# A streaming attention and channel-mix kernel: two units loaded at the start, sink values by a matmul, three PSUM banks for the channel mix, mixtures in two steps

## The chip, the cores and the metric

One Trainium2 chip, one core. The metric is the device time of one launch in microseconds; the kernel before is given as the median of three runs. The trace shows the engines TensorE (PE, its weight loads as PEld), VectorE (DVE), ScalarE (ACT), GpSimd (POOL) and the queue engine SyncE (SP). TensorE's granted clock is one of two levels, 1.2 or 2.4 GHz; the profile shows it as 0.5 or 1.0.

## What is computed

Attention in which each query sees the first 4 positions (the sinks) and the last 128 positions, and behind it a channel mix with a token shift:

```python
# q, k, v: (4, 8, 768, 64) = (batch, heads, sequence, head size)
keep = (pos_k < 4) | ((pos_q - pos_k >= 0) & (pos_q - pos_k < 128))
a = softmax(where(keep, q @ k.T / 8, -1e9))
x = heads_side_by_side(a @ v)              # (4, 768, 512)
x_prev = x shifted by one position
xk = mu_k * x + (1 - mu_k) * x_prev
xr = mu_r * x + (1 - mu_r) * x_prev
kk = relu(xk @ w_k) ** 2                   # w_k: 512 x 1024
out = sigmoid(xr @ w_r) * (kk @ w_v)       # w_r: 512 x 512, w_v: 1024 x 512
```

## The kernel before

The work is cut into 12 units of 256 positions, three to a batch entry (T = 0, 1, 2), each unit into four pairs of heads. The main loop runs over n = 4 * unit + pair. The order of every engine's instructions is the order in which they are written.

One pass of the loop issues `scores(n)` (L190: keys times queries into the two-bank tile `sc`; ScalarE takes the exponential, L194, into `e`), every second pass `mix`, then `masked(n)` (VectorE multiplies `e` by a 0/1 mask, L200 or L203), `values(n - 1)` (L216 for the sinks, L227 for the window, into the tile `o`; VectorE divides into `x`, L231 and L232), `prepare(u + 1, part)` (TensorE transposes keys or queries of the next unit, L151, ScalarE copies them out, L154; GpSimd casts the values of v, L156), and, in between, two or three chunks of the channel mix of an earlier unit (`fill`, `ffn`). `mix` (two halves a unit) transposes `x` (L247), copies it to `xt` (ACT, L253), takes the difference to the previous position `td` (L255) and makes two slices of `xk` and two of `xr` (L261), all one behind the other on VectorE.

The channel mix of a unit is 10 chunks: four of `xk @ w_k` (L274; ReLU on ACT, L278, square on DVE, L279), two of `xr @ w_r` (L286, tanh L289), and twice two halves of `kk @ w_v` (L294), each pair closed by the product `o_sb` on DVE (L299) and a store. In this text f0 to f3 are the first four chunks, r0 and r1 the next two, v0a, v0b, v1a, v1b the last four. Their results go to eight `mm` tiles a unit, which take turns in two PSUM banks. PSUM has eight banks here: two for `sc`, two for `tps` (all transposes and the sink scores), two for `o`, two for `mm`.

The unit lag is such that f0 of unit u runs in pass 4u + 6, one pass behind the second half of `mix` of that unit, and the `o_sb` of the unit before it are in pass 4u + 5.

At the start, unit 0 is loaded by SP (six loads of 256 KB in pieces of 256 bytes, L69), then eight small loads (L110) bring the sink rows of v, all batches, to `vs4`; then unit 1 is loaded. `w_k` is loaded by GpSimd's queue early, `w_r` and `w_v` behind the first work of unit 0. In pass 4 VectorE halves `w_v` into `wv_h` (L348, eight instructions). The sink rows of v are spread to `vsink` by GpSimd once a batch entry (L163).

Of the kernel before, what the change touches and what calls it, by code (L numbers as in the profile page):

```python
# [17 lines left out]
def kernel(  # L18
# [14 lines left out]
    nc = tc.nc  # L33
    B, H, S, D = q.shape
# [95 lines left out]
    hmask = const.tile([32, H, D + 1], FP32, name="hmask")  # L130
# [10 lines left out]
    def prepare(u, part):  # L141
        b, T = divmod(u, NT)
        ks, qs, vs = raw[u]
        g = part % 2
        if part == 0:
            kts[u] = kt_pool.tile([128, 2, NP, 128], BF16, name="kt")
            qts[u] = kt_pool.tile([128, NP, 256], BF16, name="qt")
        src, dst = ((ks, kts[u][:, g, :, :]), (qs, qts[u][:, :, 128 * g:128 * g + 128]))[part // 2]
        ps = tr_ps.tile([128, NP, 128], FP32, name="tps")
        for c in range(NP):  # L150
            nc.tensor.transpose(out=ps[:, c, :],  # L151
                                in_=src[:, g, 2 * c:2 * c + 2, :].rearrange("p a d -> p (a d)"),
                                identity=ident32)
# [3 lines left out]
        if part == 2 and T == 0:  # L157
# [78 lines left out]

    mixed = {}

    def mix(u, half):
# [11 lines left out]
        cur = xt[:, c0:c0 + 2, t0:t0 + 256]  # L251
        prv = xt[:, c0:c0 + 2, t0 - 1:t0 + 255]
        nc.scalar.copy(out=cur, in_=ps)  # L253
        td = x_pool.tile([128, 2, 256], BF16, name="td")
        nc.vector.tensor_tensor(out=td, in0=cur, in1=prv, op=ALU.subtract)  # L255
        if half == 0:
            mixed[u] = (x_pool.tile([128, NC, 256], BF16, name="xk"),
                        x_pool.tile([128, NC, 256], BF16, name="xr"))
        for dst, mu in zip(mixed[u], (mu_k_sb, mu_r_sb)):
            for i in range(2):  # L260
                nc.vector.scalar_tensor_tensor(  # L261
                    out=dst[:, c0 + i, :], in0=td[:, i, :], scalar=mu[:, c0 + i:c0 + i + 1],
                    in1=prv[:, i, :], op0=ALU.mult, op1=ALU.add)
# [50 lines left out]
    def fill(n, count=1):
        if n >= LAG:
            for _ in range(count):
                next(chunks, None)

    with tc.manual_schedule():
        for part in range(4):  # L320
            prepare(0, part)
        load(1)
        nc.gpsimd.dma_start(out=wr_sb, in_=moe_w_r.rearrange("(c p) f -> p c f", p=128))
        nc.gpsimd.dma_start(out=wv_sb, in_=moe_w_v.rearrange("(c p) f -> p c f", p=128))
        for n in range(N + LAG):
# [5 lines left out]
            if 2 <= n < N + 2 and c % 2 == 1:
                mix((n - 2) // NP, ((n - 2) % NP) // 2)
            fill(n)
            if n < N:
# [52 lines left out]
```

## Time and profile before

| | before |
|---|---|
| runs | 222.0, 222.08, 222.2 us, median 222.08 |
| profiled execution | 222.13 us, of which 220.4 us from first to last instruction |
| PE busy | 180.1 us (82%) |
| DVE busy | 140.9 us (64%) |
| ACT busy | 124.9 us (57%) |
| POOL busy | 34.4 us (16%) |
| chain that ended last | PE 50%, DVE 16%, ACT 12%, DMA 11%, SP's queue 5%, issue 4% |

PE is busy most of the time, but the shares are means over two stages that differ: the first 40 us, in which loads decide, and the rest, in which a unit follows a unit. An idle time in the trace has behind it the instruction that ended it.

### The profile page before, as it was taken

How to read it: one execution, taken by the hardware profiler on the slowest of the kernel's cores; microseconds unless marked ns; L12 is line 12 of the kernel's file. 1: busy time of each engine (PE TensorE's matmuls, PEld its weight loads, DVE VectorE, ACT ScalarE, POOL GpSimd, SP SyncE). 2: the span in 40 equal slices, each digit the busy share in tenths (PEclk: the TensorE clock that was granted, in tenths of full speed). 3: DMA queues.
4: the chain of work that ended last, by engine and by line, in shares of the span. 5: the costliest groups of instructions: out<-in, count | busy, mean ns of one | idle time of the engine just before them, and what ended most of it. 6: DMA issues, size and time to landing. Idle time of an engine off the chain costs nothing.

```text
span 220.4 us, 4299 instructions
## 1 busy us (share of the span) xinstructions
PE 180.1 (82%) x1664; PEld 120.9 (55%) x1664; DVE 140.9 (64%) x344; ACT 124.9 (57%) x201; POOL 34.4 (16%) x69
## 2 busy tenths in 40 slices
PE   1705706999898898996997998988998989979892
PEld 1403405675765755854755757657557557555550
DVE  0011634976786678659669757857866696697632
ACT  2402703694675675774764956855757748555250
POOL 8736011223002001032020020050020200000000
PEclk9999985799999999999999999999999999999998
DMA  7979999950591991951782945915908911020202
GB/s 128 213 142 220 179 221 209 221 97 3 146 202 37 218 166 49 216 120 49 179 157 97 206 83 150 210 26 154 222 24 213 156 49 48 3 95 0 75 23 95
DMA packets 81668, 28.10 MB, mean 127 GB/s; under 512 B 76528, under 2 KB 78064, under 8 KB 81648
## 3 DMA queue, kind: packets, MB, share of 16 engines
q1 hardware_dynamic: 78496, 25.20, 52.6%
q0 software_dynamic: 2096, 2.62, 6.9%
q8 instruction: 13, 0.21, 0.4%
q10 hardware_dynamic: 1056, 0.00, 0.3%
q14 instruction: 7, 0.06, 0.1%
HBM read 24.15 MB, written 6.29 MB: 138 GB/s over the span
## 4 chain that ended last, share of the span: by engine, by line
PE 50%; DVE 16%; ACT 12%; DMA 11%; SPq 5%; issue 4%; ACTq 0%; DVEq 0%
PE mm L274 19%; PE mm L286 9%; DMA ks<-in_k_dram 6%; PE tps L151 6%; PE mm L294 6%; DVE xr L261 5%; SPq L69 4%; DMA vs<-in_v_dram 4%; ACT e L194 4%; DVE xk L261 4%; DVE o_sb L299 3%; PE sc L190 3%; ACT xt L253 3%; ACT rl L278 3%; DVE td L255 3%
## 5 line engine op out<-in xcount | busy, mean ns | idle before, releaser
L274 PE MATMUL mm<-xk,wk_sb 128*128 128x256 bf16 x384 | 50.1, 275 | 12.9 <-DVE o_sb L299 8.5
L194 ACT ACTIVATE e<-sc 128x1024 bf16<-128x1024 f32 (+1 forms) x48 | 46.0, 958 | 9.0 <-PE sc L190 9.0
L294 PE MATMUL mm<-wv_h,kk 128*128 128x512 bf16 x192 | 48.3, 379 | 0.0
L274 PEld LDWEIGHTS <-wk_sb 128*128 128x128 bf16 x384 | 36.4, 98 | 19.1 <-issue 14.6
L278 ACT ACTIVATE rl<-mm 128x512 bf16<-128x512 f32 x48 | 29.1, 607 | 29.2 <-PE mm L274 29.2
L156 POOL CAST v<-vs 128x512 bf16<-128x512 f32 x24 | 15.9, 664 | 139.5 <-DMA vs<-in_v_dram 83.7
L154 ACT CAST kt<-tps 128x512 bf16<-128x512 f32 x24 | 14.1, 586 | 41.5 <-PE tps L151 41.5
L255 DVE TENSOR_TENSOR td<-xt 128x512 bf16<-128x512 bf16 x24 | 10.6, 440 | 40.1 <-ACT xt L253 40.1
L151 PE MATMUL tps<-ident,ks 128*128 128x128 f32 x96 | 17.4, 312 | 20.1 <-DMA ks<-in_k_dram 20.1
L151 PEld LDWEIGHTS tps<-ident,ks 128*128 128x128 f32 x96 | 13.4, 161 | 24.3 <-issue 15.3
L286 PE MATMUL mm<-wr_sb,xr 128*128 128x512 bf16 x96 | 24.4, 380 | 0.0
L294 PEld LDWEIGHTS <-kk 128*128 128x128 bf16 x192 | 16.9, 98 | 13.1
L261 DVE SCALAR_TENSOR_TENSOR xk<-td,mu_k_sb,xt 128x256 bf16<-128x256 bf16 x48 | 23.2, 524 | 0.9
L279 DVE TENSOR_TENSOR kk<-rl 128x512 bf16<-128x512 bf16 x48 | 20.2, 421 | 5.4 <-ACT rl L278 3.9
L227 PE MATMUL o<-v,e 128*128 128x65 bf16 x352 | 21.0, 196 | 1.9 <-DVE e L203 1.3
L203 DVE TENSOR_TENSOR e<-e,mask 128x768 bf16<-128x768 bf16 x16 | 8.8, 551 | 21.5 <-ACT e L194 21.5
L200 DVE TENSOR_TENSOR e<-e,mask 128x1024 bf16<-128x1024 bf16 x32 | 22.3, 697 | 0.0
L261 DVE SCALAR_TENSOR_TENSOR xr<-td,mu_r_sb,xt 128x256 bf16<-128x256 bf16 x48 | 21.7, 492 | 0.0
L227 PEld LDWEIGHTS <-e 128*128 128x128 bf16 x352 | 17.7, 99 | 7.0 <-DVE e L200 1.9
L232 DVE TENSOR_TENSOR x<-o,rec 128x256 bf16<-128x256 f32 x48 | 20.4, 424 | 1.6
L190 PE MATMUL sc<-qt,kt 64*128 64x128 bf16 (+1 forms) x256 | 19.1, 251 | 0.7 <-ACT qt L154 0.7
L299 DVE SCALAR_TENSOR_TENSOR o_sb<-th,mm 128x512 f32<-128x512 f32 x24 | 16.2, 678 | 3.5 <-PE mm L294 3.5
(42 smaller groups left out, 166.6 us busy)
## 6 DMA issues: line engine op xcount, KB each, us to landing
ks<-in_k_dram SPq DMA_DIRECT2D x24, 256.0 KB
qs<-in_q_dram SPq DMA_DIRECT2D x24, 256.0 KB
vs<-in_v_dram SPq DMA_DIRECT2D x24, 256.0 KB
out_dram<-o_sb SPq DMA_DIRECT2D x24, 256.0 KB
wk_sb<-in_moe_w_k_dram POOLq DMA_DIRECT2D x1, 1024.0 KB, 9.7
wv_sb<-in_moe_w_v_dram POOLq DMA_DIRECT2D x1, 1024.0 KB, 13.9
wr_sb<-in_moe_w_r_dram POOLq DMA_DIRECT2D x1, 512.0 KB, 7.9
vs<-in_v_dram SPq DMA_DIRECT2D x8, 4.0 KB
```

The costliest lines, as they stand in the source:

```text
L151: nc.tensor.transpose(out=ps[:, c, :], in_=src[:, g, 2 * c:2 * c + 2, :].rearrange("p a d -> p (a d)"), identity=ident32)
L190: nc.tensor.matmul(out=sc[:, a, o0:o1], lhsT=lhs[rows], rhs=qt[rows, c, q0:q0 + o1 - o0], start=True, stop=True)
L194: nc.scalar.activation(out=e[:, :, lo:], in_=sc[:, :, lo:], func=AF.Exp, scale=scale)
L200: nc.vector.tensor_tensor(out=e, in0=e, in1=mask.rearrange("p a g k q -> p a (g k q)"), op=ALU.mult)
L227: nc.tensor.matmul(out=o[:, g, a, :], lhsT=e[:, a, e0:e0 + 128], rhs=rhs, start=(T == 0 and i == 0), stop=(i == len(blocks) - 1), skip_gro ...
L232: nc.vector.tensor_tensor(out=xs[u][:, :, 128 * c:128 * c + 128].rearrange("p g (a d) -> p g a d", a=2), in0=o[:, :, :, 0:D], in1=rec.to_b ...
L261: nc.vector.scalar_tensor_tensor(out=dst[:, c0 + i, :], in0=td[:, i, :], scalar=mu[:, c0 + i:c0 + i + 1], in1=prv[:, i, :], op0=ALU.mult, ...
L274: nc.tensor.matmul(out=ps[:, i, :], lhsT=wk_sb[:, c, 128 * f:128 * f + 128], rhs=xk[:, c, :], start=(c == 0), stop=(c == NC - 1), skip_gro ...
L278: nc.scalar.activation(out=rl, in_=ps, func=AF.Relu)
L286: nc.tensor.matmul(out=ps, lhsT=xr[:, c, 128 * g:128 * g + 128], rhs=wr_sb[:, c, :], start=(c == 0), stop=(c == NC - 1))
L294: nc.tensor.matmul(out=ps, lhsT=kk[:, f, 128 * g:128 * g + 128], rhs=wv_h[:, f, :], start=(f == 0), stop=(f == NF - 1))
L299: nc.vector.scalar_tensor_tensor(out=o_sb, in0=th[g], scalar=1.0, in1=ps, op0=ALU.add, op1=ALU.mult)
```

## The change

SP loads units 0 and 1 one behind the other; the eight small loads are gone. The sink rows of v are taken from the cast values of unit T = 0 of each batch entry: a matmul with a 0/1 matrix `spread` copies rows 0 to 3 of all heads to 32 rows in a `tps` bank, and VectorE multiplies them by `hmask` into `vsink` (`sink_values`), in place of GpSimd's L163. `o` has one bank and `mm` three. `mix` is split: `transposed` (PE and ACT) stands where `mix` stood, `td` and `xk` follow `values` of the same pass, and `xr` follows one pass later. The four parts of `prepare(1)` run together in pass 3 in place of one a pass, the copies to `ksink` are made in part 3 in place of 2, `wr_sb` and `wv_sb` are asked for at the end of pass 0, and `wv_h` is made in pass 5 in place of 4.

```diff
-    o_ps = ctx.enter_context(tc.tile_pool(name="o_ps", bufs=2, space=PSUM))
-    mm_ps = ctx.enter_context(tc.tile_pool(name="mm_ps", bufs=2, space=PSUM))
+    o_ps = ctx.enter_context(tc.tile_pool(name="o_ps", bufs=1, space=PSUM))
+    mm_ps = ctx.enter_context(tc.tile_pool(name="mm_ps", bufs=3, space=PSUM))
...
     load(0)
+    load(1)
...
-    for h in range(H):
-        nc.sync.dma_start(out=vs4[4 * h:4 * h + 4, :, 0:D],
-                          in_=v[:, h, 0:NS, :].rearrange("b s d -> s b d"))
...
+    def sink_values(b):
+        ps = tr_ps.tile([128, H, D], FP32, name="tps")
+        nc.tensor.matmul(out=ps, lhsT=spread, rhs=v_bufs[b * NT % 3][:, 0, :, 0:D],
+                         start=True, stop=True)
+        nc.vector.tensor_tensor(out=vsink[b % 2][0:32, :, 0:D], in0=ps[0:32], op=ALU.mult,
+                                in1=hmask[:, :, 0:D])
...
+            if c % 2 == 1 and 2 <= n < N + 2:
+                transposed((n - 2) // NP, ((n - 2) % NP) // 2)
+            if n >= 6:
+                fill()
+            if inner:
                 masked(n)
             if 1 <= n < N + 1:
                 values(n - 1)
+            if c % 2 == 1 and 2 <= n < N + 2:
+                mix((n - 2) // NP, ((n - 2) % NP) // 2, 0)
+            if n >= 6:
+                fill()
+            if inner and u + 1 < U:
+                if u == 0 and c == 3:
+                    for part in range(4):
+                        prepare(1, part)
+                elif u > 0:
+                    prepare(u + 1, c)
                 if c == 3 and u + 2 < U:
                     load(u + 2)
+            if c % 2 == 0 and 3 <= n < N + 3:
+                mix((n - 3) // NP, ((n - 3) % NP) // 2, 1)
+            if c == 2 and inner and u % NT == 0:
+                sink_values(u // NT)
```

What this moves is seen in three places. The first is VectorE at the border of two units, in the pass in which unit u - 1 ends its channel mix: `o_sb`, then the mask `e`, `rec` and `x`, then the second `o_sb`, and `kk` of f0. Before:

```order
L232 TENSOR_TENSOR x<-o,rec 128x2x128
L255 TENSOR_TENSOR td<-xt_140 128x512
L261 SCALAR_TENSOR_TENSOR xk<-td,mu_k_sb,xt_140 128x256 x2
L261 SCALAR_TENSOR_TENSOR xr<-td,mu_r_sb,xt_140 128x256 x2
L299 SCALAR_TENSOR_TENSOR o_sb<-th,mm 128x512
L200 TENSOR_TENSOR e<-e,mask 128x1024
L231 RECIPROCAL rec<-o 128x4
L232 TENSOR_TENSOR x<-o,rec 128x2x128
L299 SCALAR_TENSOR_TENSOR o_sb<-th,mm 128x512
L279 TENSOR_TENSOR kk<-rl 128x512
```

And with the change (the line numbers are those of the changed kernel):

```order
L277 SCALAR_TENSOR_TENSOR xr<-td,mu_r_sb,xt_140 128x256 x2
L315 SCALAR_TENSOR_TENSOR o_sb<-th,mm 128x512
L207 TENSOR_TENSOR e<-e,mask 128x1024
L238 RECIPROCAL rec<-o 128x4
L239 TENSOR_TENSOR x<-o,rec 128x2x128
L273 TENSOR_TENSOR td<-xt_140 128x512
L277 SCALAR_TENSOR_TENSOR xk<-td,mu_k_sb,xt_140 128x256 x2
L315 SCALAR_TENSOR_TENSOR o_sb<-th,mm 128x512
L295 TENSOR_TENSOR kk<-rl 128x512
```

The first `o_sb` stood behind `td`, `xk` and `xr`; now it stands ahead of `td` and `xk`, and the `xr` ahead of it is that of the other half. The `xr` of this half comes two rows of `kk` later.

The second place is TensorE at f0 of a unit, with what its instructions wait for. Before:

```order
L274 LDWEIGHTS wk_sb
L274 MATMUL mm<-xk,wk_sb 128x256 [waits DVE_49]
L274 LDWEIGHTS wk_sb
L274 MATMUL mm<-xk,wk_sb 128x256
L274 LDWEIGHTS wk_sb
```

With the change:

```order
L290 MATMUL mm<-xk,wk_sb 128x256
L290 LDWEIGHTS wk_sb
L290 MATMUL mm<-xk,wk_sb 128x256
L290 LDWEIGHTS wk_sb
L290 MATMUL mm<-xk,wk_sb 128x256 [waits DVE_49]
L290 LDWEIGHTS wk_sb
L290 MATMUL mm<-xk,wk_sb 128x256 [waits DVE_49]
```

The wait on VectorE stood at f0's first matmul, which needs a bank that `o_sb` empties; now it stands at the third and the fourth, which need the two `xk` slices of the second half.

The third place is VectorE in passes 4 to 6. Before:

```order
L200 TENSOR_TENSOR e<-e,mask 128x1024
L231 RECIPROCAL rec<-o 128x4
L232 TENSOR_TENSOR x<-o,rec 128x2x128
L348 TENSOR_SCALAR wv_h<-wv_sb 128x512 x8
L255 TENSOR_TENSOR td<-xt_140 128x512
```

With the change:

```order
L273 TENSOR_TENSOR td<-xt_140 128x512
L277 SCALAR_TENSOR_TENSOR xk<-td,mu_k_sb,xt_140 128x256 x2
L376 TENSOR_SCALAR wv_h<-wv_sb 128x512 x8
L295 TENSOR_TENSOR kk<-rl 128x512
L207 TENSOR_TENSOR e<-e,mask 128x1024
L238 RECIPROCAL rec<-o 128x4
```

The eight `wv_h` instructions stood ahead of the second half of `mix` of unit 0; now they stand between it and the first `kk`.

## Rows read from the trace of the kernel before

**Rows 1.** The page's first line.

```profile
span 220.4 us, 4299 instructions
```

**Rows 2.** Waits of the whole run: us in total, times, longest us.

```profile
DVE td L255 <- ACT xt L253: 40.1, 24, 3.1
...
PE tps L151 <- DMA ks<-in_k_dram: 20.1, 4, 8.2
...
PE mm L274 <- DVE o_sb L299: 8.5, 11, 1.4
...
PE mm L274 <- ACT rl L278: 4.4, 10, 0.6
```

**Rows 3.** Busy time by engine in one unit, from f1 to f1.

```profile
72.73:87.97 15.24, 14.29 (x138) 9.81 (x138) 11.28 (x29) 10.39 (x17) 1.24 (x2) 1.00 0.69 139
```

**Rows 4.** Timeline, VectorE at a border of units: start us, us.

```profile
67.94 0.43 DVE L255 TENSOR_TENSOR td<-xt 128x512 bf16<-128x512 bf16 x1 [1.78 <-ACT xt L253]
...
68.40 1.11 DVE L261 SCALAR_TENSOR_TENSOR xk<-td,mu_k_sb,xt 128x256 bf16<-128x256 bf16 x2
...
69.43 0.87 DVE L261 SCALAR_TENSOR_TENSOR xr<-td,mu_r_sb,xt 128x256 bf16<-128x256 bf16 x2
...
70.22 0.67 DVE L299 SCALAR_TENSOR_TENSOR o_sb<-th,mm 128x512 f32<-128x512 f32 x1
70.82 0.54 DVE L203 TENSOR_TENSOR e<-e,mask 128x768 bf16<-128x768 bf16 x1
...
71.29 0.17 DVE L231 RECIPROCAL rec<-o 128x4 f32<-128x4 f32 x1
71.49 0.42 DVE L232 TENSOR_TENSOR x<-o,rec 128x256 bf16<-128x256 f32 x1
...
73.73 0.42 DVE L232 TENSOR_TENSOR x<-o,rec 128x256 bf16<-128x256 f32 x1
```

**Rows 5.** Timeline, TensorE at the same border.

```profile
66.53 1.03 PE L294 MATMUL mm<-wv_h,kk 128*128 128x512 bf16 x4
...
69.83 0.34 PE L190 MATMUL sc<-qt,kt 64*128 64x256 bf16 x4
70.95 1.03 PE L274 MATMUL mm<-xk,wk_sb 128*128 128x256 bf16 x8 [0.78 <-DVE o_sb L299]
...
72.73 1.03 PE L274 MATMUL mm<-xk,wk_sb 128*128 128x256 bf16 x8 [0.56 <-ACT rl L278]
...
74.40 0.40 PE L247 MATMUL tps<-ident,x 128*128 128x128 bf16 x4
```

**Rows 6.** Timeline, GpSimd and VectorE, where GpSimd writes vsink.

```profile
99.07 1.43 POOL L163 TENSOR_TENSOR vsink<-hmask,vs 32x520 bf16<-32x520 f32 x1
99.49 1.70 DVE L261 SCALAR_TENSOR_TENSOR xk<-td,mu_k_sb,xt 128x256 bf16<-128x256 bf16 x2
```

**Rows 7.** Timeline, GpSimd's cast of v at the border of rows 4.

```profile
67.28 1.56 POOL L156 CAST v<-vs 128x512 bf16<-128x512 f32 x2 [14.11 <-DMA vs<-in_v_dram]
```

**Rows 8.** Stretches of 2 us: PE, PEld, DVE, ACT, POOL; PEclk, DMA share, GB/s.

```profile
12.00:14.00 2.00, 0.00 (x0) 0.00 (x0) 0.17 (x1) 0.00 (x0) 0.00 (x0) 1.00 1.19 253
14.00:16.00 2.00, 0.00 (x0) 0.00 (x0) 0.00 (x0) 0.00 (x0) 1.64 (x3) 1.00 0.20 35
16.00:18.00 2.00, 0.00 (x0) 0.00 (x0) 0.00 (x0) 0.00 (x0) 1.86 (x5) 1.00 0.71 162
```

**Rows 9.** Timeline, SP's queue: the small loads, and unit 2's first.

```profile
6.90 8.49 SPq L110 DMA_DIRECT2D vs<-in_v_dram  x8
...
20.88 10.68 SPq L69 DMA_DIRECT2D ks<-in_k_dram  x2
```

**Rows 10.** Timeline, VectorE and TensorE where unit 2's keys arrive.

```profile
28.13 0.36 PE L227 MATMUL o<-v,e 128*128 128x65 bf16 x6 [1.29 <-DVE e L203]
...
33.15 2.12 DVE L348 TENSOR_SCALAR wv_h<-wv_sb 128x512 bf16<-128x512 bf16 x8 [3.38 <-DMA wv_sb<-in_moe_w_v_dram]
...
35.12 1.09 PE L151 MATMUL tps<-ident,ks 128*128 128x128 f32 x4 [6.63 <-DMA ks<-in_k_dram]
```

More of the change, by code (lines that the diff above doesn't have):

```diff
@@ L129 @@
         nc.gpsimd.memset(t, 0.0)
-    hmask = const.tile([32, H, D + 1], FP32, name="hmask")
+    hmask = const.tile([32, H, D + 1], BF16, name="hmask")
     nc.gpsimd.memset(hmask, 1.0)
@@ L135 @@
                             pattern=[[4, H], [0, D + 1]], channel_multiplier=-1)
-    nc.gpsimd.memset(vs4[:, :, D:D + 1], 1.0)
+    for t in vsink:
+        nc.gpsimd.tensor_copy(out=t[0:32, :, D:D + 1], in_=hmask[:, :, D:D + 1])
+    spread = const.tile([128, 128], BF16, name="spread")
+    nc.gpsimd.memset(spread, 0.0)
+    nc.gpsimd.tensor_copy(out=spread[0:NS, 0:4 * H].rearrange("p (h s) -> p h s", s=NS),
+                          in_=ident[0:NS, 0:NS].unsqueeze(1).to_broadcast([NS, H, NS]))
     kts, qts = {}, {}
@@ L156, in prepare @@
             nc.gpsimd.tensor_copy(out=v_bufs[u % 3][:, g, :, 0:D], in_=vs[:, g, :, :])
-        if part == 2 and T == 0:
+        if part == 3 and T == 0:
             kz = ksink[b % 2].rearrange("p (c w) -> p c w", w=136)
@@ L162, in prepare @@
                                       in_=kts[u][rows, 0, :, 0:NS])
-            nc.gpsimd.tensor_tensor(
-                out=vsink[b % 2][0:32, :, :], op=ALU.mult, in0=hmask,
-                in1=vs4[:, b:b + 1, :].to_broadcast([32, H, D + 1]))
+    def sink_values(b):
[4 more added lines that the diff above has]
+                                in1=hmask[:, :, 0:D])
     es, xs, live = {}, {}, {}
@@ L237, with transposed @@
     mixed = {}
-    def mix(u, half):
+    def transposed(u, half):
         b, T = divmod(u, NT)
@@ L250, in mix @@
         t0 = 2 + 256 * T
-        cur = xt[:, c0:c0 + 2, t0:t0 + 256]
+        nc.scalar.copy(out=xt[:, c0:c0 + 2, t0:t0 + 256], in_=ps)
+    def mix(u, half, which):
+        b, T = divmod(u, NT)
+        xt = xts[b % 2]
+        c0 = 2 * half
+        t0 = 2 + 256 * T
         prv = xt[:, c0:c0 + 2, t0 - 1:t0 + 255]
[L253 to L256, printed above, removed]
+        if half == 0 and which == 0:
             mixed[u] = (x_pool.tile([128, NC, 256], BF16, name="xk"),
[L258 to L263, printed above, removed]
+                        x_pool.tile([128, NC, 256], BF16, name="xr"),
+                        x_pool.tile([128, NC, 256], BF16, name="td"))
+        td = mixed[u][2][:, c0:c0 + 2, :]
+        if which == 0:
+            nc.vector.tensor_tensor(out=td, in0=xt[:, c0:c0 + 2, t0:t0 + 256], in1=prv,
+                                    op=ALU.subtract)
+        dst, mu = mixed[u][which], (mu_k_sb, mu_r_sb)[which]
+        for i in range(2):
+            nc.vector.scalar_tensor_tensor(
+                out=dst[:, c0 + i, :], in0=td[:, i, :], scalar=mu[:, c0 + i:c0 + i + 1],
+                in1=prv[:, i, :], op0=ALU.mult, op1=ALU.add)
     def ffn(u):
         b, T = divmod(u, NT)
-        xk, xr = mixed[u]
+        xk, xr, _ = mixed[u]
         kk = kk_pool.tile([128, NF, 256], BF16, name="kk")
@@ L310, with fill @@
     chunks = stream()
-    LAG = 6
     N = U * NP
[L314 to L319, printed above, removed]
+    def fill(count=1):
+        for _ in range(count):
+            next(chunks, None)
+    ORDERED = None
+    with tc.manual_schedule(engines=ORDERED):
         for part in range(4):
             prepare(0, part)
[L322 to L325, printed above, removed]
+        for n in range(N + 6):
             u, c = divmod(n, NP)
-            if n < N:
+            inner = n < N
+            if inner:
                 if c == 0 and u % NT > 0:
@@ L330 @@
                 scores(n)
[L331 to L334, printed above, removed]
+            if c % 2 == 1 and 2 <= n < N + 2:
+                transposed((n - 2) // NP, ((n - 2) % NP) // 2)
+            if n >= 6:
+                fill()
+            if inner:
                 masked(n)
@@ L337 @@
                 values(n - 1)
-            fill(n)
-            if n < N and u + 1 < U:
-                prepare(u + 1, c)
+            if c % 2 == 1 and 2 <= n < N + 2:
[8 more added lines that the diff above has]
+                    prepare(u + 1, c)
                 if c == 3 and u + 2 < U:
                     load(u + 2)
-            if c % 2:
-                fill(n)
-            if n == 4:
+            if c % 2 == 0 and 3 <= n < N + 3:
+                mix((n - 3) // NP, ((n - 3) % NP) // 2, 1)
+            if c == 2 and inner and u % NT == 0:
+                sink_values(u // NT)
+            if c % 2 and n >= 6:
+                fill()
+            if n == 0:
+                nc.gpsimd.dma_start(out=wr_sb, in_=moe_w_r.rearrange("(c p) f -> p c f", p=128))
+                nc.gpsimd.dma_start(out=wv_sb, in_=moe_w_v.rearrange("(c p) f -> p c f", p=128))
+            if n == 5:
                 for f in range(NF):
```

1 line of the change is left out of this document (removed).

## The prediction

> **What bounds the kernel now.** I read the list of waits first, then the timeline at one border of two units, then the first 40 us in stretches of 2 us.
>
> From about 42 us on, the profile repeats unit by unit. In the unit from f1 to f1 that the table by engine shows, TensorE is busy 14.29 of 15.24 us [rows 3]; VectorE has 11.28 and ScalarE 10.39, so TensorE is the bound and 0.95 us a unit is idle. The list of waits says where: f0 and f1 wait for `o_sb` 8.5 us in 11 waits and for the ReLU 4.4 us in 10 [rows 2]. Together that is 12.9 us, at eleven borders of units. The timeline of one border shows the mechanism. v0b ends at 66.53 + 1.03 = 67.56 us [rows 5], but its `o_sb` starts at 70.22, because VectorE first does `td`, `xk` and `xr`, and `td` itself had waited 1.78 us for ScalarE's copy into `xt` [rows 4]. f0 needs the bank that this `o_sb` empties and waits 0.78 us; f1 needs the bank of the second `o_sb` and the ReLU and waits 0.56 [rows 5]. The 40.1 us for which `td` waits for `xt` [rows 2] are VectorE's idle time with work standing behind it.
>
> The first 35 us are another stage. TensorE's last work before the gap starts at 28.13, and it goes on at 35.12, when the keys of unit 2 have landed, after 6.63 us of waiting [rows 10], one of four waits for keys with 20.1 us in all [rows 2]. The transfer engines are busy all that time (share 1.19 from 12 to 14 us) but for a hole: 0.20 from 14 to 16 and 0.71 from 16 to 18 [rows 8]. The hole is where SP had been held for 8.49 us by the eight small loads, until 15.4 us [rows 9], so that unit 1 was asked for only when unit 0 had landed.
>
> **The change, part by part.**
>
> *Third bank and split mixtures: minus 12.9.* With three banks f0 takes a bank that was emptied long before, f1 the one that the first `o_sb` empties, f2 that of the second. f1 starts 0.87 us of matmuls and more after f0, so both named waits go: -12.9 us.
>
> *What is late next: f0's third and fourth matmul, +2.6.* They need `xk` of the second half, which now stands behind `o_sb`, mask, `rec`, `x` and `td`. From v0b's end: `o_sb` to mask 0.60, mask to `rec` 0.47, `rec` to `x` 0.20, `x` 0.42, `td` to `xk` 0.46, a pair of such mixtures 0.87 (the `xr` pair; the `xk` pair beside it was disturbed), and two hand-overs of 0.06 (`o_sb` ends at 70.89, f0 starts at 70.95) [rows 4, 5]. That is 3.14 us, so `xk` is whole at 70.70. TensorE is through with the scores at 69.83 + 0.34 = 70.17 [rows 5], and the fourth matmul of a chunk of eight in 0.87 us comes 0.33 later, at 70.50. The wait is 0.20 us; the third matmul, whose slice is done about 0.42 earlier, does not wait. In units with sinks both sides are somewhat longer, and I take 0.20 for ten borders. Where the last units have no `prepare` between v1a and v1b, some 0.4 us of cover is missing, so 0.60 for one: 10 x 0.20 + 0.60 = 2.6 us. The bounds are 0 (a shorter path) and 0.6 at each border (6.6).
>
> *The transposes behind f1: +2.0.* Their second pair needs `x`, and the chain to it (f0, ReLU, `kk`, mask, `rec`, `x`) does not get shorter: f0 starts at 70.95, `x` ends at 73.73 + 0.42 = 74.15, that is 3.20 later [rows 4]. TensorE needs from f0 to the transposes 74.40 - 70.95 - 0.56 = 2.89 us without f1's wait [rows 5], and the second pair comes about 0.1 after that. So f1's old wait had covered some 0.2 us, which now shows: 10 x 0.20 = 2.0 us. Bounds: 0 and 0.4 each.
>
> *The sink values: +0.75, and a gain already counted.* The trace has no such matmul; four of 512 columns take 1.03 us [rows 5], so one is at most 0.26, with no TensorE work beside it: 3 x 0.25 = 0.75 us for the three after the start. Below, 0.2 each; above, 0.5, if the weight load shows. The VectorE product (nearest: `x` 0.42 and `o_sb` 0.67 [rows 4]) stands behind `xr`, in a place with 1 us of slack; without that cover it costs up to 0.67 each. GpSimd's product goes: while it ran (1.43 us), the pair of `xk` took 1.70 in place of 0.87 [rows 6], and this 0.83 is part of the longest wait for `o_sb`, 1.4 us [rows 2]; it is in the 12.9.
>
> The GPSIMD Engine Reference of the Trainium skill (Key points) says that GpSimd shares its SBUF interfaces with VectorE and contends with instructions that have two SBUF inputs. Rows 6 agree, and so do rows 4 and 7: `xk` took 1.11 while a cast of v ran. By the rule the casts, which stay, go on costing, so the border chain would be 0.24 longer, the rival B below.
>
> *One bank for `o`: 0.* `values(n)` must now wait until VectorE has read `values(n - 1)`. In the pass at the border, `x` follows the mask that `values(n)` needs anyway by 0.62 us (`rec` and `x` [rows 4]), and the next `values` stand behind a chunk of 0.87 and, as a rule, `prepare`, scores and another chunk, about 3 us. I find at least 1 us of slack in each of the four passes of a unit. Uncovered, it would cost 0.62 plus two hand-overs, some 0.7 us a pass.
>
> *The start: -1.5.* With load(1) directly behind load(0) the hole closes: (1.19 - 0.20) x 2 + (1.19 - 0.71) x 2 = 2.9 us at share 1.19, or 2.5 us of full work [rows 8]. If the rest of the traffic is the same, unit 2's keys land at about 32.6 in place of 35.12. Running the four parts of `prepare(1)` together costs nothing: before, TensorE had begun the last of that work at 28.13 [rows 10], 4.5 us ahead of the new time of those keys, and it has no more to do now. But `wv_h`, 2.12 us on VectorE [rows 10], was hidden in TensorE's wait; now it stands between `xk` and the first `kk`, ahead of the mask and `x` that the transposes of pass 7 need. I give back 1.0 of the 2.5 for it. Bounds: 0 (all 2.1 us shown, and 0.4 lost elsewhere) and -2.5. GpSimd's initial work changes by some tenths, under its wait for v.
>
> **Sum.** 220.4 [rows 1] - 12.9 + 2.6 + 2.0 + 0.75 - 1.5 = 211.35 us of span. The profiled execution took 222.13 us, 1.73 more than its span; the runs' median is 222.08, so they agree. 211.35 + 1.73 = **213.1 us**.
>
> **Rivals.**
>
> A. *Less comes back than I fear.* No new waits at f0 or the transposes, and all of the hole: 220.4 - 12.9 + 0.75 - 2.5 + 1.73 = 207.5 us. Against it: both waits come out of rows, with little room.
>
> B. *The VectorE chain takes most of it.* The casts of v collide with the border chain (1.11 against 0.87 [rows 4, 7]), so f0 waits 0.45 at each of eleven borders (5.0), the transposes 0.4 at ten (4.0), and the start gives nothing because `wv_h` shows in full: 220.4 - 12.9 + 5.0 + 4.0 + 0.75 + 1.73 = 219.0 us.
>
> C. *The one bank for `o` decides.* Perfetto Trace Analysis of the Trainium skill (Matmuls) says that independent matmul groups should rotate through banks, so that emptying one overlaps the next group's matmuls; the change gives up just this for `o`. As a mechanism of this kernel: if VectorE falls behind by more than the 1 us of slack, every `values` waits. At 0.4 us in each of 44 passes it is 17.6 us: 213.1 + 17.6 = 230.7. From 0.2 us a pass on (213.1 + 8.8) the kernel is no faster than before. Against it: other groups stand between two `values`, and VectorE has 4 us idle in a unit [rows 3].
>
> D. *The early load isn't early.* SP is held also by the transfers themselves: the two key loads of unit 2 took 10.68 us to be issued [rows 9]. If load(1) is held until unit 0 has landed, the hole stays and 1.5 us with it: 214.6 us. It lies within the range of the forecast.
>
> **How the numbers follow.** 0.65 for the forecast (209 to 217, D within it), 0.07 for A's end, 0.16 for B, 0.08 for C, 0.04 for no change. The range: at the low end A without its last piece, 209; at the high end between the forecast and B's 219.0, 218.0. This leaves out A's tail, C and a part of B, some 2 in 10. About 0.2% (0.4 us) is what a measurement of this kernel tells from no change. Faster: 0.65 + 0.07 + 0.15 = 0.87; the same: 0.04; slower: C and a piece of B, 0.09.
>
> **What the changed profile would show.** Waits of f0 and f1 for `o_sb` and the ReLU gone from the list; in their place f0 on `xk`, 0.1 to 0.3 us at each border, and the transposes on `x`. `td` no longer waiting for `xt` for 40 us. A unit of TensorE 14.5 to 14.9 us long from f1 to f1. No transfer share under 1 from 4 to 30 us, and unit 2's keys at 32 to 33.5 us. The prediction is wrong if `values` shows waits for `x` (C), if `xk` pairs above 1 us stand at most borders with f0 waiting (B), or if the keys of unit 2 land at 35 us as before (D).

## The result and the profile after

The kernel with the change takes 210.06 us (median of four runs, 209.30 to 211.88) against 222.14 us for the kernel before beside it: ratio 0.946, 95% interval 0.941 to 0.951, or 12.1 us less. The forecast was 213.1, its range 209 to 218. The profiled execution is the slowest of the four, 211.88 us with a span of 210.2; the spans of the other three are about 2 us shorter, probably for the reason given at the end of this section. The page's first lines:

```profile
span 210.2 us, 4310 instructions
...
PE 182.6 (87%) x1668; PEld 121.6 (58%) x1668; DVE 140.5 (67%) x348; ACT 125.7 (60%) x201; POOL 30.7 (15%) x68
```

The waits of the whole run (us in total, times, longest us), of which I show TensorE's:

```profile
PE tps L154 <- DMA ks<-in_k_dram: 13.5, 3, 8.7
...
PE o L234 <- POOL v L159: 4.0, 2, 3.1
...
PE tps L254 <- DVE x L239: 1.7, 8, 0.6
...
PE tps L254 <- ACT qt L157: 0.7, 3, 0.2
...
PE mm L290 <- DVE xk L277: 0.5, 1, 0.5
```

The waits of f0 and f1 for `o_sb` and the ReLU [rows 2] are gone, and so are the 40.1 us for which `td` waited for `xt`. In their place stand waits of the transposes (line 254), as forecast, and some 0.7 us for the copy `qt`, which was not. The remaining rows belong to the start: the keys; the 4.0 us for v, which lie ahead of 17 us, where TensorE before waited for unit 1's keys (8.2 us, [rows 2]); and the 0.5 us for `xk`, which are f0 of unit 0, at 38.91.

The timeline of VectorE at the border that answers to rows 4 (start us, us; in brackets the idle time before):

```profile
66.63 0.69 DVE L315 SCALAR_TENSOR_TENSOR o_sb<-th,mm 128x512 f32<-128x512 f32 x1 [1.13 <-PE mm L310]
...
67.23 0.72 DVE L210 TENSOR_TENSOR e<-e,mask 128x768 bf16<-128x768 bf16 x1
...
68.08 0.42 DVE L239 TENSOR_TENSOR x<-o,rec 128x256 bf16<-128x256 f32 x1
...
68.42 0.42 DVE L273 TENSOR_TENSOR td<-xt 128x512 bf16<-128x512 bf16 x1
...
68.87 0.88 DVE L277 SCALAR_TENSOR_TENSOR xk<-td,mu_k_sb,xt 128x256 bf16<-128x256 bf16 x2
...
69.67 0.68 DVE L315 SCALAR_TENSOR_TENSOR o_sb<-th,mm 128x512 f32<-128x512 f32 x1
```

The first `o_sb` now follows its matmuls at once and stands ahead of `td` and `xk`. From the end of the matmuls that it reads (65.57 + 1.03 = 66.60, the first row below) to the end of `xk` (69.75) are 3.15 us; the prediction had added up 3.14. TensorE at the same border, and the sink matmul of this unit:

```profile
65.57 1.03 PE L310 MATMUL mm<-wv_h,kk 128*128 128x512 bf16 x4
...
68.87 0.34 PE L197 MATMUL sc<-qt,kt 64*128 64x256 bf16 x4
...
69.14 1.37 PE L290 MATMUL mm<-xk,wk_sb 128*128 128x256 bf16 x8
...
70.53 1.04 PE L290 MATMUL mm<-xk,wk_sb 128*128 128x256 bf16 x8
71.41 0.60 PE L154 MATMUL tps<-ident,qs 128*128 128x128 f32 x4
71.84 0.38 PE L169 MATMUL tps<-v,spread 128*128 128x512 bf16 x1
...
72.73 0.38 PE L254 MATMUL tps<-ident,x 128*128 128x128 bf16 x4 [0.23 <-ACT qt L157]
```

f0 starts 0.27 us after the scores (before 1.12, [rows 5]). Its wait for `xk` is too short to be listed: it is hidden in the row, 1.37 us in place of 1.04. f1 follows f0 by 1.39 us (before 70.95 to 72.73, 1.78). A border without the sink matmul, in the unit behind it:

```profile
83.88 1.11 PE L290 MATMUL mm<-xk,wk_sb 128*128 128x256 bf16 x8
...
85.18 1.04 PE L290 MATMUL mm<-xk,wk_sb 128*128 128x256 bf16 x8
...
87.35 0.28 PE L254 MATMUL tps<-ident,x 128*128 128x128 bf16 x2 [0.15 <-DVE x L239]
87.47 0.71 PE L290 MATMUL mm<-xk,wk_sb 128*128 128x256 bf16 x5
```

Starts tell more than the list of waits. Over the nine whole borders, f0(2) to f0(10), counted on both traces:

| from the start of ... to the start of ... | before, us | after, us | difference |
|---|---|---|---|
| the scores ahead of f0, to f0 | 10.46 | 2.75 | -7.71 |
| f0, to f1 | 16.00 | 12.06 | -3.94 |
| f1, to f2 | 17.29 | 21.01 | +3.72 |

That is -7.93 us. From f0(1) to f0(11), ten units, the time goes from 151.73 (55.82 to 207.55) to 142.02 us (55.08 to 197.10), which is -9.71. The nine borders are 7.93 of it. Another 1.45 lie behind the last of them, from f2(10) to f0(11) (197.91 to 207.55 before, 188.91 to 197.10 after), where the trace of before has two waits that are gone:

```profile
202.39 0.30 PE L227 MATMUL o<-v,e 128*128 128x65 bf16 x4 [0.44 <-DVE e L200]
...
207.55 3.65 PE L274 MATMUL mm<-xk,wk_sb 128*128 128x256 bf16 x32 [0.85 <-DVE o_sb L299]
```

From f0(1) to f2(1) it is 0.15, and the last 0.2 lie ahead of the scores of the three units with a sink matmul. Behind f0(11) the changed kernel needs 0.25 us more (13.10 for 12.85).

The start, in stretches of 2 us (PE, PEld, DVE, ACT, POOL; PEclk, DMA share, GB/s):

```profile
12.00:14.00 2.00, 0.00 (x1) 0.10 (x1) 0.68 (x2) 0.81 (x1) 0.00 (x0) 1.00 1.21 258
14.00:16.00 2.00, 0.27 (x2) 0.16 (x2) 0.00 (x0) 0.00 (x0) 1.61 (x3) 1.00 1.38 220
16.00:18.00 2.00, 1.43 (x15) 0.75 (x14) 0.64 (x3) 0.81 (x1) 1.94 (x7) 1.00 1.37 216
...
40.00:42.00 2.00, 2.00 (x18) 1.61 (x17) 1.67 (x7) 0.60 (x1) 1.35 (x1) 0.50 0.89 187
```

And its timeline, SP's queue, TensorE and VectorE:

```profile
6.76 7.20 SPq L69 DMA_DIRECT2D ks<-in_k_dram  x2
...
18.89 10.51 SPq L69 DMA_DIRECT2D ks<-in_k_dram  x2
...
33.63 1.09 PE L154 MATMUL tps<-ident,ks 128*128 128x128 f32 x4 [8.73 <-DMA ks<-in_k_dram]
...
39.18 1.69 DVE L376 TENSOR_SCALAR wv_h<-wv_sb 128x512 bf16<-128x512 bf16 x8
...
41.00 1.87 PE L290 MATMUL mm<-xk,wk_sb 128*128 128x256 bf16 x8
41.20 0.42 DVE L295 TENSOR_TENSOR kk<-rl 128x512 bf16<-128x512 bf16 x1 [0.33 <-ACT rl L294]
```

The hole of rows 8 is closed (share 1.38 and 1.37 for 0.20 and 0.71), and unit 2's keys are used at 33.63 instead of 35.12. But the granted clock, which had fallen to 0.50 (1.2 GHz) while TensorE waited for them, stayed there until 42.7 us (before: until 41.2), so f1 of unit 0 took 1.87 us for 1.04. In the experiment e5 below, the same program but for two banks, the keys come at 32.96, the clock is back at 2.4 GHz at 36 us, and f0(1) is at 52.74 instead of 55.08. Of these 2.3 us the keys are 0.7, and the rest lies behind them. This is what the profiled execution (span 210.2) is longer than e5's (208.1). The other runs of the change have spans of 207.6 to 208.4, so they probably began like e5's, 3 us ahead of the start before (55.82); no trace shows it, and three of e5's own six runs took 211.0 to 211.2 us.

### The profile page after: what moved, and what is told of

The parts are those of the page before. It is cut to its first block, busy times and chain, and to the rows that moved or that the text cites. A ratio compares the mean times of both kernels' runs of the same rounds, so it can differ in the third digit from the quotient of the medians.

```text
span 210.2 us, 4310 instructions
## 1 busy us (share of the span) xinstructions
PE 182.6 (87%) x1668; PEld 121.6 (58%) x1668; DVE 140.5 (67%) x348; ACT 125.7 (60%) x201; POOL 30.7 (15%) x68
## 4 chain that ended last, share of the span: by engine, by line
PE 63%; DVE 10%; SPq 8%; DMA 8%; ACT 7%; issue 2%; ACTq 0%; DVEq 0%
PE mm L310 18%; PE mm L290 15%; PE mm L302 10%; SPq L69 8%; DMA ks<-in_k_dram 7%; PE tps L154 6%; PE sc L197 5%; PE o L234 3%; ACT e L201 3%; PE tps L254 3%; ACT rl L294 3%; DVE e L207 3%; DVE x L239 2%; DVE kk L295 2%; PE tps L181 2%
## 5 line engine op out<-in xcount | busy, mean ns | idle before, releaser
L290 PE MATMUL mm<-xk,wk_sb 128*128 128x256 bf16 x384 | 52.7, 278 | 0.8 <-DVE xk L277 0.5
L290 PEld LDWEIGHTS <-wk_sb 128*128 128x128 bf16 x384 | 35.2, 99 | 8.3 <-issue 3.1
L159 POOL CAST v<-vs 128x512 bf16<-128x512 f32 x24 | 16.9, 708 | 135.2 <-DMA vs<-in_v_dram 106.6
L234 PE MATMUL o<-v,e 128*128 128x65 bf16 x352 | 21.6, 198 | 4.3 <-POOL v L159 4.0
L234 PEld LDWEIGHTS <-e 128*128 128x128 bf16 x352 | 18.5, 101 | 8.7 <-issue 3.8
L277 DVE SCALAR_TENSOR_TENSOR xk<-td,mu_k_sb,xt 128x256 bf16<-128x256 bf16 x48 | 21.6, 490 | 0.8
L197 PEld LDWEIGHTS <-kt 64*128 64x128 bf16 x256 | 9.0, 96 | 15.2 <-issue 14.7
```

Source lines behind the costliest of these rows:

```text
L197: nc.tensor.matmul(out=sc[:, a, o0:o1], lhsT=lhs[rows], rhs=qt[rows, c, q0:q0 + o1 - o0], start=True, stop=True)
L234: nc.tensor.matmul(out=o[:, g, a, :], lhsT=e[:, a, e0:e0 + 128], rhs=rhs, start=(T == 0 and i == 0), stop=(i == len(blocks) - 1), skip_gro ...
L277: nc.vector.scalar_tensor_tensor(out=dst[:, c0 + i, :], in0=td[:, i, :], scalar=mu[:, c0 + i:c0 + i + 1], in1=prv[:, i, :], op0=ALU.mult, ...
L290: nc.tensor.matmul(out=ps[:, i, :], lhsT=wk_sb[:, c, 128 * f:128 * f + 128], rhs=xk[:, c, :], start=(c == 0), stop=(c == NC - 1), skip_gro ...
```

## The experiments

Ratios are to the kernel before, run beside each. f0(n) is the start of f0 of unit n; "ten units" is the time from f0(1) to f0(11).

### e1 to e4: the parts one at a time

e1_banks, the kernel before with only the banks changed:

```diff
-    o_ps = ctx.enter_context(tc.tile_pool(name="o_ps", bufs=2, space=PSUM))
-    mm_ps = ctx.enter_context(tc.tile_pool(name="mm_ps", bufs=2, space=PSUM))
+    o_ps = ctx.enter_context(tc.tile_pool(name="o_ps", bufs=1, space=PSUM))
+    mm_ps = ctx.enter_context(tc.tile_pool(name="mm_ps", bufs=3, space=PSUM))
```

> The kernel before with one bank for o and three for mm, and nothing else changed. Theory 1 (the prediction: the idle time at a border is the wait for a bank): f0 and f1 no longer wait, so the 12.9 us go, about 2 come back at the transposes, and where VectorE reads x late, behind td, xk and xr, values waits for the one bank of o, some 0.6 us in one pass of a unit: about 216 to 217 us, and values shows waits for x. Rival (the split is what counts, since the late o_sb is the cause): 219 to 222 us.

Measured: 222.46 us, ratio 1.0005 (0.998 to 1.003), so the 216 to 217 of the first theory failed. Waits, and TensorE and VectorE at the border:

```profile
PE o L216 <- DVE x L232: 11.8, 13, 1.5
...
PE o L227 <- DVE x L232: 3.4, 5, 1.3
```

```profile
70.85 0.88 DVE L261 SCALAR_TENSOR_TENSOR xr<-td,mu_r_sb,xt 128x256 bf16<-128x256 bf16 x2
...
72.92 0.42 DVE L232 TENSOR_TENSOR x<-o,rec 128x256 bf16<-128x256 f32 x1
...
73.40 0.35 PE L227 MATMUL o<-v,e 128*128 128x65 bf16 x6 [0.60 <-DVE x L232]
```

f0 and f1 wait for nothing any more, but `values` now waits 15.2 us for `x`: the one `o` bank is emptied by an instruction behind `td`, `xk` and `xr`. Rival C's mechanism is real, and in this order of VectorE's work it costs all that the third bank gives. The run tests this exchange of one bank for another, and not a third bank by itself.

e2_split, the kernel before with `mix` in the three steps of the change and the banks left at two and two; e3_banks_split, with both:

```diff
...
-                mix((n - 2) // NP, ((n - 2) % NP) // 2)
+                transposed((n - 2) // NP, ((n - 2) % NP) // 2)
...
             if 1 <= n < N + 1:
                 values(n - 1)
+            if c % 2 == 1 and 2 <= n < N + 2:
+                mix((n - 2) // NP, ((n - 2) % NP) // 2, 0)
...
+            if c % 2 == 0 and 3 <= n < N + 3:
+                mix((n - 3) // NP, ((n - 3) % NP) // 2, 1)
```

> The kernel before with mix in three steps (transposes where they were, td and xk behind values, xr one pass later), two banks for o and two for mm as before, start as before. Theory 1 as I made the sum: o_sb now stands ahead of td and xk, so the bank for f0 is empty in time and f1 waits little; about 213.5 to 215 us, as good as the two together. Rival (banks are what counts): f0 still waits for a bank and 218 us or more.

> The kernel before with both of these. By the prediction's terms: 222.1 - 12.9 + 2.6 + 2.0 = 213.8 us, and the sum of the gains of banks alone and split alone is more than this, since both take away the same wait. If the gain from the start and from the sink values is larger than I took (the profile of the changed kernel has shorter waits at f0 than I took): 212 to 213 us.

Measured: e2 212.88 us, 0.958 (0.955 to 0.962); e3 213.02 us, 0.959 (0.955 to 0.963). The waits of e2:

```profile
PE tps L247 <- DVE x L232: 3.4, 13, 0.6
PE mm L283 <- DVE xk L270: 0.9, 2, 0.5
```

No wait for `o_sb` is left with two banks either. The split gives 9.4 us by itself. The third bank, paid for with one of `o`'s, gives nothing without it, and nothing that shows with it (the intervals are some 0.8 us to either side). The waits of f0 and f1 end without another bank: the place of `o_sb` in VectorE's queue is enough.

e4_sink_start, the changed kernel with `mix` in one piece and the banks as before (two and two), so only the early load and the sink matmul:

> The changed kernel with two banks for o, two for mm and mix in one piece as before: only the start and the sink values by matmul are left of the change. By the prediction's terms -1.5 us at the start, +0.75 for three matmuls, and -0.8 at each of three borders where GpSimd's product ran beside xk: about 219 us. Rival (the start gives nothing, the eight wv_h stand in the way): 220.5 us, and keys of unit 2 at 33 to 34 us with the second chunk of unit 0's channel mix no earlier than before.

Measured: 222.99 us, 1.002 (0.999 to 1.004). My expectation, 219, failed. Ten units take 151.91 us (before 151.73): what the sink matmul gives it also takes. At two borders f0's wait for `o_sb` falls from 1.35 to 0.54 us, since GpSimd's product no longer runs beside `xk`; at the three borders with the sink matmul the way from f1 to f2 grows from 1.91 to 2.42. At the start the keys came at 34.34, but f0(1) is at 56.44, later than before:

```profile
40.75 2.15 DVE L363 TENSOR_SCALAR wv_h<-wv_sb 128x512 bf16<-128x512 bf16 x8
...
42.82 0.41 DVE L286 TENSOR_TENSOR kk<-rl 128x512 bf16<-128x512 bf16 x1
...
44.44 0.28 PE L254 MATMUL tps<-ident,x 128*128 128x128 bf16 x2 [1.78 <-DVE x L239]
```

This is the give-back of the prediction, near its upper bound of 2.1: `wv_h`, then `kk`, mask, `rec` and `x`, and the transposes wait 1.78 us.

### e5 to e7: the parts taken back one at a time

e5_two_mm_banks, the changed kernel with e1's edit undone (`o` 2, `mm` 2):

> The changed kernel with two banks for o and two for mm, as the kernel before has them; all the rest of the change stays. Theory after the first four runs (the third bank is worth nothing once o_sb stands ahead of td and xk): the same as the changed kernel, 210 us, no wait of f0 or f1 for o_sb. Rival (the prediction's text: f0 and f1 are freed by the third bank): 213 us or more, with waits for o_sb in the list.

Measured: 210.41 us, 0.945 (0.941 to 0.948), ten units 142.22 us (142.02 with the change). The third bank and the single `o` bank show no effect, in either direction.

e6_sink_by_pool, the changed kernel with GpSimd's product in place of the sink matmul, and the small loads that it needs behind load(1):

```diff
...
-        ps = tr_ps.tile([128, H, D], FP32, name="tps")
-        nc.tensor.matmul(out=ps, lhsT=spread, rhs=v_bufs[b * NT % 3][:, 0, :, 0:D],
-                         start=True, stop=True)
-        nc.vector.tensor_tensor(out=vsink[b % 2][0:32, :, 0:D], in0=ps[0:32], op=ALU.mult,
-                                in1=hmask[:, :, 0:D])
+        nc.gpsimd.tensor_tensor(
+            out=vsink[b % 2][0:32, :, :], op=ALU.mult, in0=hmask,
+            in1=vs4[:, b:b + 1, :].to_broadcast([32, H, D + 1]))
```

> The changed kernel with the sink rows of v by eight small loads as before, asked for behind load(1), and spread by GpSimd's product, which is issued at the place of the matmul (pass 2 of a batch entry, not at the border). Theory: unit 1 is still asked for early, three matmuls (0.25 us each and a wait of about as much for their bank) are saved, and the product runs beside other VectorE work off the border: 209.5 to 210.5 us, as the changed kernel. Rival (it is the matmul in place of GpSimd's product that gives the part of the gain that the start and the split don't explain): 211.5 us or more, with the pair of xk or another pair of mixtures near 1.7 us in three places and TensorE waiting for it.

Measured: 213.12 us, 0.959 (0.955 to 0.963): 2.7 us more than e5; in the traces 1.6 of them are in ten units (143.85 us) and 1.2 ahead of f0(1) (53.96), where the keys came 1.2 later (34.18 for 32.96) and both then need 19.78 us. My expectation failed. GpSimd and VectorE:

```profile
64.78 1.30 POOL L158 CAST v<-vs 128x512 bf16<-128x512 f32 x2 [13.93 <-PE tps L251]
...
66.04 1.19 POOL L167 TENSOR_TENSOR vsink<-hmask,vs 32x520 bf16<-32x520 f32 x1
...
66.13 1.52 DVE L207 TENSOR_TENSOR e<-e,mask 128x768 bf16<-128x768 bf16 x1
...
69.11 1.10 PE L287 MATMUL mm<-xk,wk_sb 128*128 128x256 bf16 x6 [0.68 <-DVE xk L274]
```

I had thought the product was off the border, because its call stands where the sink matmul does, behind f1. But GpSimd has nothing else to do and starts the product right behind the casts of v, at the border, where the mask took 1.52 us (0.55 undisturbed, at 71.28 of this run; 0.72 at the border shown above, where a cast of v ran beside it), `xk` came later and f0 waited 0.68. At the other two borders of this kind the mask took 1.27 and 1.08 us. So this run shows the price of the collision, not that of another place. In e3, with the product in its old place, the same stands at two borders: f0 to f1 takes 2.06 and 2.20 us there, 1.22 to 1.30 at most others. The Trainium skill's GPSIMD Engine Reference (Key points) has GpSimd contend for SBUF with VectorE instructions that have two SBUF inputs, as the mask has; the rows agree, 1.52 us beside 0.55.

e7_wvh_pass4, the changed kernel with `wv_h` one pass earlier, where VectorE waits for the keys anyway:

```diff
-            if n == 5:
+            if n == 4:
```

> The changed kernel with the eight wv_h in pass 4 in place of 5. The prediction's term: wv_h in pass 5 gives back 1.0 us at the start, so 209.0 us. Rival, by the changed kernel's timeline (after wv_h the first kk waits 0.33 us for ScalarE, so wv_h is over in time): no difference, 210 us.

Measured: 209.38 us, 0.941 (0.937 to 0.944). That lies between what I expected and the rival, and its interval meets that of the change, so the times do not decide. From the keys to f0(1) it needs 20.03 us (32.55 to 52.58), e5 19.78 (32.96 to 52.74): in these two traces `wv_h` in pass 5 costs nothing. In e8, below, it does.

### e8 to e12: the start

e8_warm and e10_warm_wvh4 (the second with e7's edit too) put 32 matmuls, whose result nothing reads, into the gap ahead of unit 2's keys, so that TensorE's clock does not fall:

```diff
+                    if n == 4:
+                        warm = tr_ps.tile([128, 512], FP32, name="tps")
+                        for i in range(32):
+                            nc.tensor.matmul(out=warm, lhsT=ident, rhs=wk_sb[:, 0, 0:512],
+                                             start=True, stop=True)
```

> The changed kernel with 32 matmuls of 512 columns added before the first transposes of unit 2, into a PSUM tile that nothing reads; they lie in TensorE's wait for the keys of unit 2 (about 25 to 33 us, some 7 us of work at 2.4 GHz). Theory: TensorE's clock is 1.2 GHz from 29 to 42 us in the changed kernel only since TensorE stood idle before; kept busy, it works at 2.4 GHz from the keys on, and the end comes 2 to 3 us earlier, 207 to 208 us, with the granted clock at 1.00 through that stretch. Rival (that stretch is bound by loads or by ScalarE and VectorE, not by TensorE's clock): no difference, or later by what the 32 matmuls stick out.

> The 32 extra matmuls that keep TensorE busy in its wait, with the eight wv_h in pass 4. Without wv_h in the way, which in the last run with these matmuls held the transposes of pass 7 for 1.03 us, the clock at 2.4 GHz should now show: theory 207.5 to 208.5 us, about 1 us under the kernel with wv_h in pass 4 alone (209.4). Rival (VectorE and ScalarE, or loads, set the pace there): 209 to 210 us.

Measured: e8 210.59 us, 0.945 (0.942 to 0.949); e10 210.47 us, 0.944 (0.940 to 0.948). The mean granted clock was 0.996 and 1.000, and the time is that of the change: I had expected 207 to 208 of e8 and 207.5 to 208.5 of e10. TensorE, faster, waited instead. e8:

```profile
38.06 1.10 PE L290 MATMUL mm<-xk,wk_sb 128*128 128x256 bf16 x6 [1.41 <-DVE xk L277]
38.32 2.53 DVE L381 TENSOR_SCALAR wv_h<-wv_sb 128x512 bf16<-128x512 bf16 x8
...
42.40 0.28 PE L254 MATMUL tps<-ident,x 128*128 128x128 bf16 x2 [1.03 <-DVE x L239]
```

VectorE had been standing still until the keys came, as TensorE had, and its chain, with `wv_h` in it, is then what lasts longest. e10 takes `wv_h` out of the chain. Its row at the keys, and that of e7:

```profile
34.48 0.63 PE L154 MATMUL tps<-ident,ks 128*128 128x128 f32 x4 [0.66 <-DMA ks<-in_k_dram]
```

```profile
32.55 1.09 PE L154 MATMUL tps<-ident,ks 128*128 128x128 f32 x4 [6.74 <-DMA ks<-in_k_dram]
```

From the keys to f0(1) e10 needs 19.16 us (34.48 to 53.64), the least of all runs with this start; e8 needs 20.09 (33.70 to 53.79), so with TensorE at 2.4 GHz `wv_h` in pass 5 costs 0.9. Against e7, whose clock is at 1.2 GHz until 36.6 us, e10 is 0.9 shorter. But its keys came 1.9 us later than e7's. TensorE waited for them with the 32 matmuls done, so why they were late is open, and so is whether this is what keeps e10's other runs from being faster.

e9_weights_late asks for two of the weights three passes later, so that they do not go ahead of unit 2's keys, and makes `wv_h` two passes later; e11_all_weights_late also moves `wk_sb` and drops `wv_h` (the factor 0.5 goes into the ReLU's scale):

```diff
-            if n == 0:
+            if n == 3:
                 nc.gpsimd.dma_start(out=wr_sb, in_=moe_w_r.rearrange("(c p) f -> p c f", p=128))
                 nc.gpsimd.dma_start(out=wv_sb, in_=moe_w_v.rearrange("(c p) f -> p c f", p=128))
-            if n == 5:
+            if n == 7:
```

```diff
...
-    nc.gpsimd.dma_start(out=wk_sb, in_=moe_w_k.rearrange("(c p) f -> p c f", p=128))
...
-            nc.scalar.activation(out=rl, in_=ps, func=AF.Relu)
+            nc.scalar.activation(out=rl, in_=ps, func=AF.Relu, scale=0.5 ** 0.5)
...
+            if n == 0:
+                nc.gpsimd.dma_start(out=wk_sb, in_=moe_w_k.rearrange("(c p) f -> p c f", p=128))
...
```

> The changed kernel with w_r and w_v asked for at the end of pass 3, behind the casts of unit 1, in place of pass 0, and wv_h made in pass 7. Theory (the start is bound by the load engines, and what the keys of unit 2 wait for is the traffic ahead of them): 1.5 MB of w_r and w_v no longer go before them, so they land 5 to 8 us earlier, near 26 us, and a good part of that reaches the end: 205 to 207 us. Rival (what follows is bound by the same total of loads, or by wv_h in pass 7): keys near 26 us, but 209 to 211 us.

> As the first of this call, with w_k also asked for later (end of pass 0, behind the casts of unit 0), and without wv_h: the factor 0.5 goes into the ReLU as a scale of the root of 0.5. Theory (load-bound start): unit 0's v lands at 10 to 11 us in place of 14.4, unit 2's keys near 22 us, f0 of unit 0 waits for w_k at most a little, and the end comes at 200 to 204 us. Rival (total traffic to the point where the loop runs freely decides, whatever its order): no better than the first of this call.

Measured: e9 203.47 us, 0.914 (0.910 to 0.918); e11 202.38 us, 0.910 (0.906 to 0.914). e9 is below the 205 to 207 that I had expected. Ten units are as with the change (142.38 in both); all of it is the start. SP and TensorE in e9:

```profile
19.07 2.12 SPq L69 DMA_DIRECT2D ks<-in_k_dram  x2
...
25.68 0.63 PE L154 MATMUL tps<-ident,ks 128*128 128x128 f32 x4
...
26.64 11.34 SPq L69 DMA_DIRECT2D ks<-in_k_dram  x2
```

SP issues unit 2's keys in 2.12 us where the change needed 10.51, TensorE does not wait for them, and f0(1) is at 46.73. The long hold has moved to unit 3's keys, for which TensorE does not wait. e11 has f0(1) at 44.81 and is the fastest of all: faster than the kernel before and the change.

e12_sink_start_wvh4, e4 with `wv_h` in pass 4 (e7's edit):

> The kernel that has only the start and the sink values by matmul (mix in one piece, two banks each), with the eight wv_h in pass 4 in place of 5. Theory: that kernel was no faster than the one before since wv_h stood ahead of the first kk and held the transposes of pass 7 for 1.8 us, which is what the start had gained; without it 221 to 221.7 us (1.2 to 1.8 us less), and the second pair of those transposes waits less than 0.5 us. Rival (the start gains nothing, whatever wv_h does): 222.5 to 223.2 us.

Measured: 220.16 us, 0.991 (0.988 to 0.994), below what I had expected; the longest wait of the transposes for `x` falls from 1.78 to 0.19 us:

```profile
41.03 0.28 PE L254 MATMUL tps<-ident,x 128*128 128x128 bf16 x2 [0.19 <-DVE x L239]
```

From unit 2's keys to f0(1) it needs 20.51 us (32.52 to 53.03), e4 22.10 (34.34 to 56.44). So in these traces 1.6 us are `wv_h`; the other 1.8 are keys that came earlier, which the edit does not explain.

## Why the prediction was right, and where its terms were off

The sum was 3 us too high. Its mechanism, that f0 and f1 would stop waiting and the transposes begin to, is what the traces show; the terms are off in both directions. In the ten units and behind them the terms add up to -7.55 us, and the traces show -9.46 (-9.71 and +0.25); the start, by difference, gave some 2.6 of the 12.1 us in place of 1.5. That the sum is nearer than its largest terms is in part luck: more went than I had listed, and more came back. Of the signs, a unit from f1 to f1 takes 14.0 to 14.9 us, where I had 14.5 to 14.9.

**Third bank and split mixtures, -12.9.** The waits went, but the credit was wrong: I had explained f0 by a bank "emptied long before". e2 against the kernel before, and e5 against the change, show that the split does it without that bank. The size was too small too. At the border of rows 5 the list gave f0 0.78 us, while f0 came 0.85 nearer to the scores (1.12 to 0.27). On the nine borders the listed waits are 11.1 us. The first two rows of the table make 11.65, and f0's rows of after hold another 1.5 of new wait, so 13.2 were removed, 0.23 a border more than listed. The reason I would give, argued and not tested: matmuls that follow each other overlap (eight take 1.03 us, one alone 0.27, at 37.43 of e7), and a stall also loses that overlap, which the list counts as busy.

**f0 on `xk`, +2.6.** The chain was right to 0.01 us, partly by luck: from the mask to `x` it took 0.85 us for 0.67, beside a cast of v, and from `x` to `td` 0.34 for 0.42, with one hand-over of 0.03 for two of 0.06. The price was not right: over the nine borders f0's rows are 1.5 us longer than 1.04 in all, where I had 2.2 (8 x 0.20 + 0.60). At the three borders ahead of a sink matmul (as that of 69.14) it is 0.16 to 0.33, at five others 0.07. The single border without cover cost 0.50 for 0.60.

**The transposes, +2.0, and the sink matmul, +0.75.** Together +3.72 on the nine borders, where I had 9 x 0.20 + 3 x 0.25 = 2.55. At a usual border it is 0.33, since the stall is again more than the 0.15 that is listed. At the three with a sink matmul it is 0.52 (2.42 for 1.90); e2 and e3, without that matmul, need 2.33 there, so 0.09 is its price and the rest is again the transposes. In all that is some 3.45 for the transposes, where nine borders had 1.8, and 0.27 for the matmul in place of 0.75: its own 0.38 us and the wait of 0.23 for the bank that `qt`'s copy empties lie mostly in time that the transposes would have waited anyway. In the unsplit kernel, where they do not wait, it costs 0.51 (e4). VectorE's product (0.67 us) stays hidden.

**GpSimd's product, in the 12.9.** Right that it collides: e6 shows that 1.6 us of the ten units would be missing without its removal. The 1.2 at its start are keys that came later; the small loads may be the reason, but e4 and e12, with the same loads, differ by 1.8.

**One bank for `o`, 0.** Right: one wait of 0.3 us for `x` in e6 and in the change. What I had not seen is that it holds only because the split puts `rec` and `x` ahead of the mixtures: in e1 the same bank costs 15.2. The rule of the Trainium skill's Perfetto Trace Analysis (Matmuls), to rotate through banks, is borne out by e1 and costs nothing here to break.

**The start, -1.5.** f0(1) came 3.1 us earlier in e5, 0.7 in the profiled execution of the change, whose clock stayed low longer. The hole closed as forecast (rival D is out, though SP is held 7.20 us). The keys came 1.5 us earlier in the change and 2.2 in e5, for 2.5; over all traces with the early load and the weights as in the change it is 0.6 (e10) to 2.6 (e12). Behind the keys I had put 1.0 more for `wv_h`. In e5 it is 0.9 less than before (19.78 for 20.70), and e2 and e3, with the old start, have 0.4 and 0.6 of that, so a part is the split's.

The step that was too simple is the give-back as one price: `wv_h` costs nothing by e5 and e7, 0.9 by e8 and e10, and 1.6 in the unsplit kernel by e4 and e12. I had taken its place from the order of the program, and not asked how long the first `kk` would be late anyway. In the change `wv_h` ends at 40.87, and `kk` waits for the ReLU until 41.20; in e8 `wv_h` lasts 2.53 us, TensorE is faster, and `kk` waits for VectorE.

**What I had not priced at all** is the larger thing: the weights that are loaded ahead of unit 2's keys. Two of them, 1.5 MB, asked for later (with `wv_h` behind them), are 6.6 us (e9 against the change, 203.47 and 210.06), more than any other piece of the start.

**Open:** why unit 2's keys come at 32.52 in one run and at 34.34 in another with the same loads (e12 and e4), what decides when the clock comes back, what a third `mm` bank would give that is not taken from `o`, which part of the split does it (`o_sb` ahead of `td` and `xk`, or `xr` out of the way), and what e11's 1.1 us over e9 are made of (`wk_sb` later, or no `wv_h`).

## What to carry to other kernels

A wait for a bank names who empties it; look first at what stands ahead of that instruction in its engine's queue, since a bank that is taken from another tile only moves the wait (e1), while a better place in the queue ends it (e2). An instruction on an idle engine runs when its inputs come, not where its call stands, so moving the call does not move the collision (e6). And at a start that is bound by loads, ask for what is used late behind what is used first (e9).

## What the runs showed of the hardware

GpSimd's product of 32x520 beside VectorE's mask stretched that from 0.55 to 1.52 us (e6), much as the `xk` pair of rows 6. SP's issue of the same two loads of 256 KB takes 2.12 us or 10.51, without or with 1.5 MB of weights asked for ahead of them (e9 and the change). Closing the hole raised the transfer engines' share to 1.38, but at 220 GB/s, less than the 258 at share 1.21 just before: share is not bandwidth. Keeping TensorE at 2.4 GHz through its wait did not shorten the run (210.59 and 210.47 us in e8 and e10), although from the keys to f0(1) e10 was 0.9 us shorter than e7; in the profiled execution of the change 1.2 GHz until 42.7 us went with 1.7 us more from the keys to f0(1) than in e5 (21.45 for 19.78).
